# One list schedule for the whole kernel: order pinned on every engine, the halves of two chunks in turn, the positive part of the ELU on ScalarE

## The chip, the core and the metric

The kernel runs on one core of a Trainium2 chip. TensorE (PE in the profile) multiplies, VectorE (DVE), ScalarE (ACT) and GpSimd (POOL) work on tiles, and SyncE (SP) issues the DMAs. The metric is the device time of one execution in microseconds (us); the figure for a kernel is the median of its runs.

## The reference

Three stages follow one another, over 3072 tokens (4 sequences of 768) with 384 features (8 heads of 48):

```python
for t in range(S):                       # gated linear attention, per sequence and head
    state = alpha[t][:, None] * state + outer(k[t], v[t])
    y[t] = q[t] @ state
h = x @ w_in                             # 384 -> 2048
x2 = where(h > 0, h, exp(min(h, 0)) - 1) @ w_out
g = x2 @ w_gate; val = x2 @ w_val        # 384 -> 1536
out = (g * sigmoid(g) * val) @ w_out2
```

All of it is in single precision. The kernel reaches it with three passes per product (high by high, high by low, low by high) on operands that are split into a high and a low part.

## The kernel before, in words

The 768 steps are cut into 6 chunks of 128 steps. A chunk of all four sequences is a block of 512 tokens (TB), and one sequence's share of a chunk is a *unit* u = 0 to 23 (unit u belongs to chunk u // 4).

*Attention of a unit* (class `Attention`). `load` fetches one tile `in` of 1 MB with the decays F, K, Q and V; there are three such buffers, so unit u + 3 is fetched when unit u is done. `A` multiplies the decays up (a scan on DVE, four pieces), clamps them (`R`), and ACT takes the inverse by Ln and Exp. `N` and `M` scale K by a guarded inverse (the tile `N`) and Q by the decay; two of their products, K by `R` and Q by F, run on POOL (L214, L224), the others on DVE (L212, L222). `Dk` transposes K on PE (L235) and ACT keeps it as `KT`; `E` forms the scores on PE (L254) and DVE masks them into `A` (L261); `Gs` forms the new state on PE (L274, L278); `Hy` forms the outputs on PE (L299 from the state `sbd`, L304 and L308 from the scores), and ACT and DVE split them into the high and low part of `x` and of `x3`. After a chunk's fourth unit `gaps` fills the remaining rows of `x` from `x3` with six small DMAs.

*First layer* (`moe1`), for each chunk 16 steps f: nine products of 128x512 into `h` (`mm1`), the ELU on ACT and DVE (L361 to L367), whose result is split into the high and low part of `g`, and nine products into the three accumulators `acc` (`mm2`, two steps f later). *Second layer* (`moe2`), for each chunk 12 steps: 18 products into `gv`, the gate, and twelve products of 128x384 into `q`. All of these products are issued in `mm3` and so have line L117. Results of the first layer go through DRAM (`x2d`), and `load_split` brings them back.

*Weights* (class `Weight`) come in tiles of 768 KB of float64, 16 for the first layer and 18 for the second. A tile passes through one of two `raw` buffers: two conversions on ACT (L91, L93), two merges on DVE (L95, L98), and a split into high and low, one instruction on ACT (L105) and one on DVE (L106). One tile of the first layer is prepared at each step f of chunk 0, three before it.

*What sets the order.* The code emits the work in a fixed pattern: 30 products of zeros to begin with, the attention of chunk 0, then the first layer of chunk c with the attention of chunk c + 1 cut into 28 pieces and dealt out over its steps (`POPS`). From that the framework's scheduler (it simulates a timeline) makes each engine's order; it is free to move instructions of one engine past each other. Each engine then runs its list strictly in order.

Of the kernel before, what the change touches and what calls it, by code (L numbers as in the profile page):

```python
# [18 lines left out]
DM = H * D  # L19
# [13 lines left out]
AHEAD = 2  # L33
EARLY = 10
POPS = [3] * 9 + [1] + [0] * 6
PASSES = ((0, 0), (0, 1), (1, 0))


@with_exitstack
def kernel(  # L40
# [9 lines left out]
    nc = tc.nc  # L50

# [3 lines left out]
    def open_pools(es, weights):  # L55
        P.wp = es.enter_context(tc.tile_pool(name="wp", bufs=weights))
        P.xp = es.enter_context(tc.tile_pool(name="xp", bufs=2))
        P.ep = es.enter_context(tc.tile_pool(name="ep", bufs=2))
        P.gp = es.enter_context(tc.tile_pool(name="gp", bufs=3))
        P.rp = es.enter_context(tc.tile_pool(name="rp", bufs=AHEAD))  # L60
        P.op = es.enter_context(tc.tile_pool(name="op", bufs=2))

    dp = ctx.enter_context(tc.tile_pool(name="dp", bufs=1, space=bass.MemoryType.DRAM))
    x2d = [dp.tile([128, KD, TB], F32, name=f"x2d{c}") for c in range(NCH)]
# [10 lines left out]


    class Weight:


        def __init__(self, pool, tag, src):  # L80
            self.t = pool.tile([128, 2, WT], F32R, tag=tag, name="wt")
            self.raw = P.rp.tile([128, WT, 2], I32, tag="raw", name="raw")
            nc.sync.dma_start(
                out=self.raw.rearrange("p a t -> p (a t)"), in_=src.bitcast(I32))

        def value(self):
# [3 lines left out]
            lo, hi = self.raw[:, :, 0], self.raw[:, :, 1]  # L90
            nc.scalar.activation(  # L91
                out=hi.bitcast(F32), in_=hi.bitcast(F32), func=AF.Copy, scale=2.0 ** -112)
            nc.scalar.activation(  # L93
                out=lo, in_=lo.bitcast(U32), func=AF.Copy, scale=0.936 * 2.0 ** -29)
            nc.vector.scalar_tensor_tensor(  # L95
                out=lo, in0=hi, scalar=3, in1=lo,
                op0=ALU.logical_shift_left, op1=ALU.bitwise_or)
            nc.vector.scalar_tensor_tensor(  # L98
# [3 lines left out]
        def split(self):  # L102
            w = self.raw[:, :, 0].bitcast(F32)
            hi, lo = self.t[:, 0], self.t[:, 1]
            nc.scalar.activation(out=hi, in_=w, func=AF.Copy)  # L105
            nc.vector.tensor_tensor(out=lo, in0=w, in1=f32(hi), op=ALU.subtract)  # L106
            del self.raw
# [7 lines left out]
    def mm3(o, lhs, rhs, first, last):  # L115
        for i, (a, b) in enumerate(PASSES):
            nc.tensor.matmul(  # L117
                out=o, lhsT=lhs(a), rhs=rhs(b),
                start=first and i == 0, stop=last and i == 2,
            )  # L120


    class Attention:
        def __init__(self, es):
            self.cp = es.enter_context(tc.tile_pool(name="acp", bufs=1))
            self.p1 = es.enter_context(tc.tile_pool(name="ap1", bufs=1))
            self.p2 = es.enter_context(tc.tile_pool(name="ap2", bufs=2))
            self.p3 = es.enter_context(tc.tile_pool(name="ap3", bufs=3))
# [12 lines left out]
            self.turn = False  # L141

        def bank(self, u=NU):

            self.turn = not self.turn
            if u < B and not self.turn:
                return pacc.tile([128, 512], F32, tag="acc2", name="acc2")
            return self.ps.tile([128, 512], F32, tag="aps", name="aps")

        def pair(self, u):  # L150

            if u < B and u % 2 == 0:
# [21 lines left out]
        def warm(self, n):  # L174

            z = self.cp.tile([128, 128], BF16, name="wz")
            nc.vector.memset(z, 0.0)
            o = pacc.tile([128, 512], F32, tag="acc2", name="acc2")
            for _ in range(n):
                nc.tensor.matmul(  # L180
                    out=o, lhsT=z, rhs=z[:, None, :].to_broadcast([128, 4, 128]), start=True, stop=True)

        def load(self, u):
            t = self.p3.tile([128, 4, NP * C], F32, tag="in", name="in")
            for i, j in ((0, 1), (1, 4)) if u == 0 else ((0, 4),):
                nc.sync.dma_start(out=t[:, i:j], in_=qkva[u][:, i:j])
            f, k, q = (t[:, i].rearrange("p (a c) -> p a c", a=NP) for i in range(3))
            self.u[u] = dict(t=t, F=f, K=k, Q=q, v=t[:, 3].rearrange("p (h d) -> p h d", h=H))

        def A(self, u):  # L190

            d = self.u[u]
            for p in range(NP):
                f = d["F"][0:PR, p]
                nc.vector.tensor_tensor_scan(  # L195
                    out=f, data0=f, data1=self.zero[0:PR].to_broadcast([PR, C]),
                    initial=1.0, op0=ALU.mult, op1=ALU.add,
                )
            r = self.p1.tile([128, NP * C], F32, tag="R", name="R")[0:PR]
            nc.vector.tensor_scalar(  # L200
                out=r, in0=d["t"][0:PR, 0], scalar1=2.0 ** -60, scalar2=2.0 ** 60,
                op0=ALU.max, op1=ALU.min)
            nc.scalar.activation(out=r, in_=r, func=AF.Ln)
            nc.scalar.activation(out=r, in_=r, func=AF.Exp, scale=-1.0)  # L204
            d["R"] = r

        def N(self, u):

            d = self.u[u]
            t = self.p1.tile([128, NP * C], F32, tag="N", name="N")[0:PR]  # L210
            f, k = d["t"][0:PR, 0], d["t"][0:PR, 1]
            nc.vector.scalar_tensor_tensor(  # L212
                out=t, in0=f, scalar=0.0, in1=d["R"], op0=ALU.max, op1=ALU.mult)
# [514 lines left out]
```

## Time and profile before

| | us |
|---|---|
| median of 3 runs (1021.95 to 1024.06) | 1022.18 |
| the profiled execution | 1022.64 |
| its span, first to last instruction | 1020.9 |
| PE busy, of the span | 980.6 |
| DVE, ACT, POOL busy | 573.5, 462.7, 86.2 |

Line numbers are those of the code above. "busy" of PE is modelled and holds time in which products only wait in its pipeline, so a span at 100% need not be at full pace; the start of a group of nine products against the start of the next is the better measure. A row of the timeline gives start, duration, engine, line, operation, result and operands, and how many instructions it merges; in brackets is the idle time ahead and what ended it.

### The profile page before, as it was taken

Reading aid. Unit: us, or ns where it says so; the run is one execution under the profiler, and the core shown is the slowest. Engines: PE = TensorE matmul, PEld = TensorE weight load, DVE = VectorE, ACT = ScalarE, POOL = GpSimd, SP = SyncE. Lnnn points to the kernel's source line nnn. Section 1 sums busy time; section 2 is a strip of 40 time slices with the busy share of each in tenths; the row PEclk is TensorE's granted clock in tenths of the full one; section 3 lists DMA queues with packets and bytes.
Section 4 is the critical chain, followed back from the end, with each engine's and each line's share of the span. In section 5 each row is a group of like instructions: output and inputs, shape, how many; then the busy total and the mean of one; then the engine's idle time right before and its main releaser. Section 6 shows DMA issues by size and latency. Waiting matters only on the chain.

```text
span 1020.9 us, 13174 instructions
## 1 busy us (share of the span) xinstructions
PE 980.6 (96%) x5248; PEld 813.9 (80%) x5248; DVE 573.5 (56%) x951; ACT 462.7 (45%) x806; POOL 86.2 (8%) x59
## 2 busy tenths in 40 slices
PE   7589999999999999999998999999999999999997
PEld 4467778877787878888776888888888888888886
DVE  6899996656665665647888433433433433433332
ACT  5678786455555455637877321211311222212121
POOL 4223111120211121100000000000000000000000
PEclk8589999999999999999999999999999999999998
DMA  5544432222112212203533100100200100100001
GB/s 227 206 160 165 165 120 74 83 57 73 43 55 75 83 42 58 73 16 125 186 124 125 62 1 1 62 1 1 62 1 1 62 1 1 62 1 22 10 0 35
DMA packets 18934, 69.36 MB, mean 68 GB/s; under 512 B 2480, under 2 KB 5552, under 8 KB 15920
## 3 DMA queue, kind: packets, MB, share of 16 engines
q1 hardware_dynamic: 18864, 68.43, 19.9%
q8 instruction: 43, 0.70, 0.3%
q14 instruction: 27, 0.22, 0.1%
HBM read 56.62 MB, written 9.44 MB: 65 GB/s over the span
## 4 chain that ended last, share of the span: by engine, by line
PE 79%; DVE 8%; DMA 7%; ACT 3%; issue 2%; SPq 0%; POOL 0%; DVEq 0%
PE gv L117 29%; PE q L117 15%; PE acc L117 14%; PE h L117 14%; DMA raw<-w 4%; DMA in<-qkva 2%; PE ape L254 2%; DVE wt L106 2%; PE aps L299 2%; PE aps L308 1%; DVE raw L98 1%; DVE raw L95 1%; DVE in L195 1%; ACT raw L93 1%; ACT raw L91 1%
## 5 line engine op out<-in xcount | busy, mean ns | idle before, releaser
L117 PE MATMUL gv<-x,wt 128*128 128x512 f32 x1296 | 310.1, 393 | 2.3 <-DVE e L364 2.3
L117 PEld LDWEIGHTS gv<-x,wt 128*128 128x128 f32 x1296 | 243.3, 189 | 51.0 <-issue 2.7
L117 PE MATMUL acc<-g,wt 128*128 128x512 f32 x864 | 224.6, 398 | 4.3 <-DVE g L367 2.4
L117 PE MATMUL h<-x,wt 128*128 128x512 f32 x864 | 220.3, 398 | 8.4 <-DVE e L364 4.2
L117 PEld LDWEIGHTS h<-x,wt 128*128 128x128 f32 x864 | 161.3, 190 | 45.5 <-DVE e L364 6.6
L117 PEld LDWEIGHTS acc<-g,wt 128*128 128x128 f32 x864 | 158.7, 188 | 44.0 <-DVE g L367 4.4
L117 PE MATMUL q<-wt,u 128*128 128x384 f32 x864 | 163.0, 337 | 0.0
L117 PEld LDWEIGHTS q<-wt,u 128*128 128x128 f32 x864 | 153.6, 188 | 5.5
L414 DVE TENSOR_TENSOR s<-gv,s 128x512 f32<-128x512 f32 x72 | 49.8, 692 | 180.9 <-ACT s L413 180.8
L413 ACT ACTIVATE s<-gv 128x512 f32<-128x512 f32 x72 | 43.1, 598 | 185.3 <-PE gv L117 185.2
L416 ACT ACTIVATE u<-s 128x512 fp32r<-128x512 f32 x72 | 45.4, 631 | 130.4 <-DVE s L415 130.4
L366 ACT ACTIVATE g<-e 128x512 fp32r<-128x512 f32 x96 | 60.2, 629 | 65.6 <-DVE e L364 64.1
L361 ACT ACTIVATE e<-h 128x512 f32<-128x512 f32 x96 | 56.7, 590 | 58.7 <-PE h L117 57.8
L367 DVE TENSOR_TENSOR g<-e,g 128x512 fp32r<-128x512 f32 x96 | 67.8, 708 | 16.5 <-ACT g L366 15.0
L363 DVE TENSOR_SCALAR e<-e 128x512 f32<-128x512 f32 x96 | 42.6, 446 | 61.2 <-ACT e L362 61.0
L417 DVE TENSOR_TENSOR u<-s,u 128x512 fp32r<-128x512 f32 x72 | 49.8, 692 | 44.0 <-ACT u L416 44.0
L415 DVE TENSOR_TENSOR s<-gv,s 128x512 f32<-128x512 f32 x72 | 49.8, 691 | 43.0 <-PE gv L117 43.0
L364 DVE SCALAR_TENSOR_TENSOR e<-h,e 128x512 f32<-128x512 f32 x96 | 65.9, 687 | 2.1
L224 POOL TENSOR_TENSOR in<-in 112x512 f32<-112x512 f32 x24 | 40.6, 1691 | 300.2 <-DVE in L195 266.5
L362 ACT ACTIVATE e<-e 128x512 f32<-128x512 f32 x96 | 59.9, 628 | 1.8
L195 DVE TENSOR_TENSOR_SCAN in<-in,zero 112x128 f32<-112x128 f32 x96 | 34.5, 415 | 26.8 <-DMA in<-qkva 26.8
L214 POOL TENSOR_TENSOR in<-in,R 112x512 f32<-112x512 f32 x24 | 43.6, 1818 | 35.7 <-ACT R L204 35.6
(88 smaller groups left out, 776.0 us busy)
## 6 DMA issues: line engine op xcount, KB each, us to landing
raw<-w SPq DMA_DIRECT2D x34, 768.0 KB, 4.3
in<-qkva SPq DMA_DIRECT2D x23, 1024.0 KB, 5.0
x2d<-o SPq DMA_DIRECT2D x18, 256.0 KB, 2.0
x2r<-x2d SPq DMA_DIRECT2D x18, 256.0 KB, 2.9
out<-y SPq DMA_DIRECT2D x24, 192.0 KB, 2.0
x<-x SPq DMA_DIRECT2D x36, 64.0 KB, 4.5
in<-qkva SPq DMA_DIRECT2D x1, 768.0 KB, 5.1
in<-qkva SPq DMA_DIRECT2D x1, 256.0 KB, 3.7
```

Of the source, the lines that this page charges most:

```text
L117: nc.tensor.matmul(out=o, lhsT=lhs(a), rhs=rhs(b), start=first and i == 0, stop=last and i == 2,)
L195: nc.vector.tensor_tensor_scan(out=f, data0=f, data1=self.zero[0:PR].to_broadcast([PR, C]), initial=1.0, op0=ALU.mult, op1=ALU.add,)
L214: nc.gpsimd.tensor_tensor(out=k, in0=k, in1=d["R"], op=ALU.mult)
L361: nc.scalar.activation(out=e, in_=h, func=AF.Relu, scale=-1.0)
L362: nc.scalar.activation(out=e, in_=e, func=AF.Exp, scale=-1.0)
L364: nc.vector.scalar_tensor_tensor(out=e, in0=h, scalar=0.0, in1=e, op0=ALU.max, op1=ALU.add)
L366: nc.scalar.activation(out=g[:, 0], in_=e, func=AF.Copy)
L367: nc.vector.tensor_tensor(out=g[:, 1], in0=e, in1=f32(g[:, 0]), op=ALU.subtract)
L414: nc.vector.tensor_tensor(out=e, in0=ps[0], in1=e, op=ALU.mult)
L415: nc.vector.tensor_tensor(out=e, in0=ps[1], in1=e, op=ALU.mult)
L416: nc.scalar.activation(out=g[:, 0], in_=e, func=AF.Copy)
L417: nc.vector.tensor_tensor(out=g[:, 1], in0=e, in1=f32(g[:, 0]), op=ALU.subtract)
```

## The change

All work is listed first, as steps of a `Plan`, each with its engine, an estimated duration, the buffers that it reads and writes, and a mark `port` for those of DVE and POOL that are to exclude one another in the plan. `run` is a list scheduler: it takes the engine that can begin first, on it the ready step with the longest chain of work behind it (`tail`; attention's products on PE get 40 us on top, and are taken as ready 0.5 us late), and emits all steps in the order of their planned starts. `Pinned` makes each instruction of an engine depend on the one before it, so the framework's scheduler keeps that order.

Other parts: the first layer of chunks 0 and 1 is done in halves, in the order chunk 0 steps 0 to 7, chunk 1 steps 0 to 7, chunk 0 steps 8 to 15, chunk 1 steps 8 to 15; the sums of the first halves go to DRAM (`half`), come back (`part`), and are added on DVE. The list puts the attention of chunk 1 with the first of these segments, that of chunk 2 with the fourth. For units 0 to 3 the two products of POOL run on DVE. The mask of scores that lie in one tile is one instruction of 128x1024. In the ELU the positive part is a second Relu on ACT into a tile `r`, and DVE forms e - 1 + r in one instruction where it had two (the subtraction of 1, L363, is gone; L364 read `h` from PSUM, the new one reads two tiles in SBUF). The output buffers are three where they were two.

```diff
-POPS = [3] * 9 + [1] + [0] * 6
+HALF = NF1 // 2
+SEGMENTS = [(0, 0, HALF, 1), (1, 0, HALF, 0), (0, HALF, NF1, 0), (1, HALF, NF1, 2)]
+SEGMENTS += [(c, 0, NF1, (c + 1) % NCH) for c in range(2, NCH)]
+SOON, MARGIN = 40.0, 0.5
+RAWS, INS, OUTS, GS = 2, 3, 3, 3
...
+    def run(self):
...
+            t, eng, at = best
+            i = max((i for i in at if at[i] <= t), key=lambda i: (tail[i] + ops[i][5], -i))
+            ready[eng].remove(i)
+            start[i], free[eng] = t, t + ops[i][1]
+            if ops[i][4]:
+                port = free[eng]
...
+        for i in sorted(range(n), key=lambda i: (start[i], i)):
+            ops[i][2]()
...
+            ins = getattr(self.engine, name)(*a, **k)
+            if self.on:
+                if self.prev is not None:
+                    self.tc.add_manual_dep(
+                        ins.ins, self.prev, mybir.DependencyInfo(
+                            mybir.DependencyClass.NoSync, mybir.DependencyReason.DATA),
+                        reason="order of the plan")
+                self.prev = ins.ins.name
...
+        def helper(self, u):
+            return pool if u >= B else vec
+        def cost(self, u):
+            return ("POOL", 1.3) if u >= B else ("DVE", 0.62)
...
-            nc.vector.tensor_scalar(out=e, in0=e, scalar1=-1.0, scalar2=None, op0=ALU.add)
-            nc.vector.scalar_tensor_tensor(
-                out=e, in0=h, scalar=0.0, in1=e, op0=ALU.max, op1=ALU.add)
+            def pos():
+                d["r"] = P.ep.tile([128, TB], F32, tag="r", name="r", bufs=1)
+                act.activation(out=d["r"], in_=d["h"], func=AF.Relu)
+            def elu():
+                vec.scalar_tensor_tensor(
+                    out=d["e"], in0=d["e"], scalar=-1.0, in1=d["r"], op0=ALU.add, op1=ALU.add)
...
+            plan.add("PE", 2.05, product, r=[w1[f // G, 0].key, *xs], w=[hk, "chain"])
+            plan.add("ACT", 0.55, pos, r=[hk], w=["r"])
+            plan.add("DVE", 0.63, elu, r=["r"], w=[ek], port=True)
...
+    for c, f0, f1, n in SEGMENTS:
+        if n:
+            for u in range(B * n, B * n + B):
+                at.step(u)
...
+        for f in range(f0, f1):
+            if (f // G, 0) not in w1:
+                prep_w1(plan, f)
+                prep_w1(plan, f + 1)
+            mm1(f)
```

The order that results, at three places. In the changed kernel every instruction of the plan has line L123, that of the wrapper. A trailing "x4" is four instructions in one row.

First, DVE up to the last part of `x` that chunk 0's first product needs (the last row of each). Before:

```order
L261 TENSOR_TENSOR A_422<-ape_411,mask_119 128x512
L106 TENSOR_TENSOR wt_472<-raw_473,wt_472 128x768
L222 SCALAR_TENSOR_TENSOR in_320<-N_424,in_320 112x512
L319 TENSOR_TENSOR x3_123<-aps_372,x3_123 112x128
L320 TENSOR_TENSOR x_185<-aps_372,x_185 112x3x128
L95 SCALAR_TENSOR_TENSOR raw_503<-raw_503 128x768
L195 SCALAR_TENSOR_TENSOR in_385<-in_385,zero_120 112x128 x4
L98 SCALAR_TENSOR_TENSOR raw_503<-raw_503 128x768
L319 TENSOR_TENSOR x3_123<-acc2_441,x3_123 112x128
L320 TENSOR_TENSOR x_185<-acc2_441,x_185 112x3x128
```

and in the changed kernel:

```order
L123 SCALAR_TENSOR_TENSOR in_338<-in_338,zero_119 112x128 x4
L123 TENSOR_SCALAR R_397<-in_338 112x512
L123 TENSOR_TENSOR wt_376<-raw_178,wt_376 128x768
L123 TENSOR_TENSOR A_408<-ape_382,mask_118 128x1024
L123 TENSOR_TENSOR x3_122<-aps_366,x3_122 112x128
L123 TENSOR_TENSOR x_257<-aps_366,x_257 112x3x128
L123 SCALAR_TENSOR_TENSOR N_426<-in_338,R_397 112x512
L123 SCALAR_TENSOR_TENSOR in_391<-in_391,zero_119 112x128 x4
L123 TENSOR_TENSOR x3_122<-acc2_417,x3_122 112x128
L123 TENSOR_TENSOR x_257<-acc2_417,x_257 112x3x128
```

Up to that point stand 14 instructions on `raw` and `wt` before (five weight tiles begun), and 3 now (one tile, whose split is the row on `wt_376`); the eight products that POOL had for units 0 to 3 are among DVE's now.

Second, PE near the eighth step of chunk 0 (`x_185` and `x_257` are chunk 0's block, `x_569` chunk 1's; the name behind it is the weight tile). Before:

```order
L117 MATMUL h_1060<-x_185,wt_738 128x512 x9
L117 MATMUL acc0_479<-g_931,wt_683 128x512
L117 MATMUL acc1_480<-g_931,wt_683 128x512
L117 MATMUL acc2_481<-g_931,wt_683 128x512
L117 MATMUL acc0_479<-g_931,wt_683 128x512 x2
L117 MATMUL acc1_480<-g_931,wt_683 128x512 x2
L117 MATMUL acc2_481<-g_931,wt_683 128x512 x2
L117 MATMUL h_1103<-x_185,wt_875 128x512 x9
L254 MATMUL ape_1322<-in_762 128x128
L117 MATMUL acc0_479<-g_994,wt_808 128x512
```

and in the changed kernel:

```order
L123 MATMUL h_947<-x_257,wt_823 128x512 x9
L123 MATMUL acc0_607<-g_923,wt_859 128x512 x3
L123 MATMUL acc1_608<-g_923,wt_859 128x512 x3
L123 MATMUL acc2_609<-g_923,wt_859 128x512 x3
L123 MATMUL h_985<-x_569,wt_376 128x512 x9
L123 MATMUL acc0_607<-g_964,wt_982 128x512 x3
L123 MATMUL acc1_608<-g_964,wt_982 128x512 x3
L123 MATMUL acc2_609<-g_964,wt_982 128x512 x3
```

After eight steps chunk 0 needs a new weight tile before (`wt_875`); now chunk 1 begins there with the first tile (`wt_376`), which has been ready since the start. Its own second half needs the next tiles sixteen groups of products later.

Third, the scores of a unit on PE (a result `ape`). Before, those of unit 7 stand in three pieces among products:

```order
L254 MATMUL ape_1322<-in_762 128x128
L117 MATMUL acc0_479<-g_994,wt_808 128x512
L117 MATMUL acc1_480<-g_994,wt_808 128x512
L117 MATMUL acc2_481<-g_994,wt_808 128x512
L254 MATMUL ape_1322<-in_762 128x128
L235 MATMUL aps_904<-ident_118,in_595 128x112 x4
L117 MATMUL acc0_479<-g_994,wt_808 128x512 x2
L117 MATMUL acc1_480<-g_994,wt_808 128x512 x2
L117 MATMUL acc2_481<-g_994,wt_808 128x512 x2
L254 MATMUL ape_1322<-in_762 128x128 x6
```

and in the changed kernel:

```order
L123 MATMUL acc0_607<-g_750,wt_693 128x512 x3
L123 MATMUL acc1_608<-g_750,wt_693 128x512 x3
L123 MATMUL acc2_609<-g_750,wt_693 128x512 x3
L123 MATMUL h_809<-x_257,wt_657 128x512 x9
L123 MATMUL aps_826<-ident_117,in_567 128x112 x4
L123 MATMUL ape_834<-in_567 128x128 x8
L123 MATMUL aps_849<-in_567,KT_843 64x48
```

They are one piece now, beside the transposition of the same unit. From the first product of the first layer on, attention stands in 78 pieces between products before, and in 53 now.

## Rows read from the trace of the kernel before

**Rows 1.** Windows by stage: length; busy PE, PEld, DVE, ACT, POOL; clock; DMA.

```profile
0.00:56.10 56.10, 34.37 (x255) 23.94 (x255) 45.27 (x83) 34.99 (x61) 19.45 (x22) 0.67 0.55 201
56.10:157.10 101.00, 97.52 (x582) 76.67 (x583) 94.16 (x154) 80.07 (x139) 20.62 (x11) 0.96 0.45 152
157.10:243.20 86.10, 86.10 (x521) 68.83 (x520) 54.68 (x105) 47.43 (x92) 15.37 (x8) 1.00 0.21 67
...
415.60:496.50 80.90, 78.53 (x417) 62.81 (x416) 51.30 (x86) 48.04 (x79) 2.98 (x2) 1.00 0.24 79
496.50:565.10 68.60, 63.31 (x262) 49.02 (x261) 55.47 (x81) 54.29 (x82) 0.00 (x0) 0.98 0.40 138
565.10:1013.50 448.40, 448.39 (x2161) 394.63 (x2159) 164.38 (x243) 103.16 (x173) 0.00 (x0) 1.00 0.06 20
1013.50:1020.90 7.40, 0.00 (x0) 0.00 (x0) 0.69 (x2) 0.37 (x1) 0.00 (x0) 0.65 0.33 115
```

**Rows 2.** Timeline of PE: the first product, one after a stall, two undisturbed.

```profile
56.09 2.90 PE L117 MATMUL h<-x,wt 128*128 128x512 f32 x6 [3.93 <-DMA x<-x]
...
79.78 3.64 PE L117 MATMUL h<-x,wt 128*128 128x512 f32 x9 [1.57 <-DVE e L364]
...
474.75 2.20 PE L117 MATMUL h<-x,wt 128*128 128x512 f32 x9
476.79 2.20 PE L117 MATMUL acc<-g,wt 128*128 128x512 f32 x9
```

**Rows 3.** Window of DVE alone, first scan to chunk 0's last part of x.

```profile
4.60:53.20 48.60, 42.23 (x73) 0.65 0.56 211
```

**Rows 4.** Timeline of DVE, an undisturbed stretch of chunk 0's attention.

```profile
41.77 0.94 DVE L106 TENSOR_TENSOR wt<-raw,wt 128x768 fp32r<-128x768 f32 x1
42.64 0.94 DVE L98 SCALAR_TENSOR_TENSOR raw<-raw 128x768 int32<-128x768 int32 x1
43.51 0.67 DVE L212 SCALAR_TENSOR_TENSOR N<-in,R 112x512 f32<-112x512 f32 x1
44.11 1.27 DVE L261 TENSOR_TENSOR A<-ape,mask 128x512 int32<-128x512 int32 x2
45.31 0.94 DVE L106 TENSOR_TENSOR wt<-raw,wt 128x768 fp32r<-128x768 f32 x1
```

**Rows 5.** Timeline of DVE beside work of POOL.

```profile
11.78 1.52 DVE L200 TENSOR_SCALAR R<-in 112x512 f32<-112x512 f32 x1
...
203.16 0.66 DVE L364 SCALAR_TENSOR_TENSOR e<-h,e 128x512 f32<-128x512 f32 x1
...
255.62 1.76 DVE L212 SCALAR_TENSOR_TENSOR N<-in,R 112x512 f32<-112x512 f32 x1
```

**Rows 6.** Timeline of POOL at the same three places.

```profile
11.76 1.26 POOL L224 TENSOR_TENSOR in<-in 112x512 f32<-112x512 f32 x1 [2.09 <-DVE in L195]
...
203.47 1.29 POOL L224 TENSOR_TENSOR in<-in 112x512 f32<-112x512 f32 x1 [14.21 <-DVE in L195]
...
255.54 1.29 POOL L214 TENSOR_TENSOR in<-in,R 112x512 f32<-112x512 f32 x1 [1.06 <-ACT R L204]
```

**Rows 7.** Timeline of PE, scores in a piece of two and in one piece.

```profile
264.21 0.49 PE L254 MATMUL ape<-in 48*128 48x128 f32 x2
264.62 2.34 PE L117 MATMUL acc<-g,wt 128*128 128x512 f32 x9
...
273.43 1.16 PE L254 MATMUL ape<-in 48*128 48x128 f32 x16
274.52 0.50 PE L117 MATMUL acc<-g,wt 128*128 128x512 f32 x1
```

**Rows 8.** The page's costliest groups: count, busy, mean ns, idle before.

```profile
L361 ACT ACTIVATE e<-h 128x512 f32<-128x512 f32 x96 | 56.7, 590 | 58.7 <-PE h L117 57.8
L214 POOL TENSOR_TENSOR in<-in,R 112x512 f32<-112x512 f32 x24 | 43.6, 1818 | 35.7 <-ACT R L204 35.6
```

**Rows 9.** Waits: engine and line, what for; us in total, times, longest.

```profile
DVE in L195 <- DMA in<-qkva: 26.8, 17, 3.6
```

More of the change, by code (lines that the diff above doesn't have):

```diff
@@ L50 @@
     nc = tc.nc
+    vec, act, pool, ten, syn = engines = [
+        Pinned(tc, e) for e in (nc.vector, nc.scalar, nc.gpsimd, nc.tensor, nc.sync)]
     class P:
@@ new lines, in split_lo @@
+        def split_lo():
+            vec.tensor_tensor(
+                out=w.t[:, 1], in0=w.raw[:, :, 0].bitcast(F32), in1=f32(w.t[:, 0]),
+                op=ALU.subtract)
+        plan.add("SP", 0.5, load, w=[hk, lk], kb=768)
+        plan.add("ACT", 0.82, high, w=[hk])
+        plan.add("ACT", 0.82, low, w=[lk])
+        plan.add("DVE", 0.88, merge, r=[hk], w=[lk], port=True)
+        plan.add("DVE", 0.88, sign, r=[hk], w=[lk], port=True)
+        plan.add("ACT", 0.82, split_hi, r=[lk], w=[w.key])
@@ L109, in as_cols @@
+        plan.add("DVE", 0.88, split_lo, r=[lk], w=[w.key], port=True)
+        return w
     def as_cols(w):
@@ new lines, in E, with scores @@
+                plan.add("ACT", 0.65, state, r=[("sc", b)], w=[("sbd", u % 2)])
+            keys, pair = self.pair(u)
+            def scores():
+                d["s"] = o = pair()
+                for p in range(NP):
+                    for j in range(2):
+                        r = slice(64 * j, 64 * j + D)
+                        ten.matmul(
+                            out=(o[j] if len(keys) > 1 else o[:, j])[:, p * C:(p + 1) * C],
+                            lhsT=d["K"][r, p], rhs=d["Q"][r, p], start=True, stop=True,
+                        )
@@ L267, in Gs @@
+            plan.add("PE", 1.25, scores, r=[K, Q], w=keys, soon=SOON, lag=MARGIN)
+            plan.add("DVE", 1.24 if len(keys) > 1 else 1.1, causal, r=keys, w=["A"])
         def Gs(self, u):
@@ L401, in mm_gv, with low, moe2 @@
+            def low(m=m, o=o):
+                vec.tensor_tensor(
+                    out=b.t[:, 1, m], in0=o.t, in1=f32(b.t[:, 0, m]), op=ALU.subtract)
+            plan.add("SP", 0.5, load, r=[(after, m)], w=[o.key])
+            xk = ("x", c % 2, m)
+            plan.add("ACT", 0.55, high, r=[o.key], w=[xk])
+            plan.add("DVE", 0.63, low, r=[o.key], w=[xk], port=True)
+        return b
+    def moe2(plan, x, xs, w2, pools, yp, put):
+        accs, us = {}, {}
         def mm_gv(f):
-            fs = slice((f % G) * 128, (f % G) * 128 + 128)
@@ new lines, in low @@
+            def low():
+                vec.tensor_tensor(
+                    out=d["g"][:, 1], in0=d["e"], in1=f32(d["g"][:, 0]), op=ALU.subtract)
+            plan.add("ACT", 0.55, sigmoid, r=[gks[0]], w=[ek])
+            plan.add("DVE", 0.63, lambda: times(0), r=[gks[0]], w=[ek])
+            plan.add("DVE", 0.63, lambda: times(1), r=[gks[1]], w=[ek])
+            plan.add("ACT", 0.57, high, r=[ek], w=[uk])
+            plan.add("DVE", 0.63, low, r=[ek], w=[uk], port=True)
+            us[f] = d, uk
```

794 lines of the change are left out of this document (468 added, 326 removed).

## The prediction, as it was made

> **What bounds the kernel now.** I read the busy shares by stage first, then PE's timeline where a stage begins, then DVE's timeline in the stage that looked worst. The stages [rows 1] are, with their lengths: the attention of chunk 0 ahead of any product of the first layer, 56.1 us; chunk 0's first layer with the attention of chunk 1, 101.0; chunks 1, 2 and 3, of which one row stands and which take 86.1, 86.2 and 86.2; chunk 4, 80.9; chunk 5, 68.6; the second layer, 448.4; and 7.4 behind it for the last output. They add up to the span of 1020.9; the execution has 1.7 us around it (1022.6), and the median of the runs is 0.5 below the profiled one.
>
> A group of nine products takes 2.04 us when nothing disturbs it (from 474.75 to 476.79) [rows 2]. The second layer takes 448.4 us with PE never free, and its order is the same in the change (18 products of `gv`, twelve of `q`): nothing is to be had there. Chunks 1 to 3 are PE's too: 32 groups make 65.3 us, the attention of four units the other 20.9, 5.2 a unit. Chunk 0 does the same work on PE in 101.0 us, 14.9 more; there DVE is busy for 94.2 of the 101.0, and in chunk 1 for 54.7 of 86.1. In the first 56.1 us PE has only attention and the clock is 0.67 of full speed in the mean, and DVE again has little left: it is busy for 42.2 of the 48.6 us [rows 3] between its first scan and the last part of `x`, at 53.2; the first product starts 2.9 us after that [rows 2]. In chunks 4 and 5 PE is free for 2.4 and 5.3 us [rows 1], because ACT and DVE prepare the second layer's weights there. So the kernel is DVE's for 157 us and PE's for nearly all of the rest.
>
> **The start.** What DVE does up to the last part of `x` changes like this (counts from the two orders, durations as steps from start to start in an undisturbed stretch [rows 4]):
> - Eleven weight instructions go behind it (14 become 3): 11 x 0.87 = 9.6 us less.
> - Eight products of POOL come to DVE. The trace does not show them there; the nearest row is the `N` of L212, also two tiles of 112x512 in SBUF, 0.60. That adds 4.8. From both sides: by the weights' 0.87 it would be 7.0, by half of the two mask instructions' 1.20, 0.60 again.
> - One product of the next unit goes behind: 0.6 less.
> - Collisions with POOL go. The clamp of 11.78 took 1.52 us and ended 0.28 us after the POOL instruction that had begun at 11.76 and took 1.26 [rows 5, 6]; it is the first of six instructions of DVE that are stretched so in this part, by 0.7 to 1.1 us, 5.6 together.
>
> 42.2 - 9.6 + 4.8 - 0.6 - 5.6 = 31.2 us of work. DVE's waits in the stretch, 48.6 - 42.2 = 6.4 us, are for ACT, PE and loads; I leave them as they are, since the chain of a unit through ACT and a PE at low clock stays and fewer fillers stand between. Then `x` is ready at 4.6 + 31.2 + 6.4 = 42.2 and the first product starts at 45.1 instead of 56.1: **-11.0 us**. Without any wait it would be 38.7 (-17.4); if the waits grow by what the work shrinks, nothing is won. POOL's idleness costs nothing there.
>
> **Chunk 0.** DVE now has, from 42.2 up to the fifth pair of `e` and `g` (from where on a step needs only that pair and a few weights), 20 weight instructions (17.4), ten of the ELU (6.0, priced as L212) and 18.7 of attention, priced alike: 42.1 us, ending at 84.3. PE's own work up to the same place is 11 groups, 22.5, and nearly four units, about 19: from 45.1 to 86.6. Without disturbance PE just sets the end. DVE has disturbances: of the 101.0 us before, 6.8 were idle and collisions of that kind with POOL's 11 products [rows 1], ten of 0.2 to 1.1 us, cost 7.6, together 14%; at that rate 42.1 becomes 49.0, the fifth pair is ready at 91.2, and PE waits for 5. Afterwards chunk 1's first half needs no new weight, and the eight tiles for the second halves spread over 66 us of products. So of the 14.9 us about 5 stay: **-9.9 us**, between -14.9 and 0.
>
> The ELU itself loses one DVE instruction (L363) and has one more on ACT, 0.59 us [rows 8]; 96 of them are 57 us on an engine that is busy for 80.1 of 101.0 us in chunk 0 and for 47.4 of 86.1 in chunk 1 [rows 1]. There it is hidden by PE. In chunk 0 the eight steps of the first segment bring ACT 4.7 us while it loses weights of the later tiles, so I count it as nothing; without cover it is 0.1 us a step, the difference of 0.59 and the subtraction that it replaces, at most 5 us on 48 steps. The twelve DMAs and six additions of the halves (one addition like a `g`, about 0.7 us) lie beside PE and a DMA share of 0.21 [rows 1]: nothing, at most 4 us if PE waited for all six additions.
>
> The new instruction reads two tiles in SBUF where L364 read `h` in PSUM. The trace shows what that exposes it to: L364 took 0.66 us beside a POOL instruction, L212, with two SBUF operands, 1.76 beside another, against 0.67 alone [rows 4 to 6]. The Trainium skill says the same (GPSIMD Engine Reference, § 8 Key points): POOL shares its SBUF interfaces with VectorE and contends with instructions that read two SBUF inputs or run in a two-port mode. By that rule each of the 40 POOL products left could hold one ELU for 1.1 us, 44 us of DVE in all. I do not add them to the sum, as the subtraction that goes was open to the same; they enter the slow rival.
>
> **Pieces.** Products of the first layer are now in whole groups. Scores in a piece of two records took 0.41 us from their start to the next group's, 16 in one piece 1.09 [rows 7]: by its share a piece of two would take 0.14, so cutting off a piece costs some 0.27. From chunk 1 on there are 41 pieces instead of 59: 18 x 0.27 = **-4.9 us**; 0 if the cost belonged to the scores alone, -7 at the whole 0.41.
>
> **Chunks 4 and 5.** PE's free 7.7 us. Before, all 18 tiles of the second layer stand ahead of its first gate on DVE; now ten do, and the rest lies among the gates, where DVE is busy for 164 of 448 us. I give back **-5**, between -7.7 and +4 (a gate queued on DVE behind a late weight; a step of 6.2 us holds about 3 us of DVE work).
>
> Sum: -11.0 - 9.9 - 4.9 - 5 = -30.8; span 990.1, execution 991.8, and 0.5 less for the median: 991.4, so **991 us**.
>
> **Rivals.**
> - *DVE never sets the end* (0.20). No collisions from POOL at the start, and the list puts urgent work first, so the 5 us of chunk 0 and the 6.4 us of waits go too: 980 us. Against it: DVE strictly keeps its list, so each late operand holds everything behind it.
> - *The start does not move* (0.21). The chain of a unit (scan, ACT, product, PE, mask, PE) or the loads, for which scans waited 17 times and 3.6 us at worst [rows 9], set chunk 0's attention, and the eight products that come to DVE lie in that chain. Then the first term is gone: 1002; with chunk 0 no better either, 1012.
> - *The plan's margins are too small* (0.08), the slow side. Attention's products on PE are put 0.5 us behind the planned end of their inputs and ahead of everything else. The plan has 1.3 us for a POOL product that took 1.82 in the mean [rows 8]; two of them and a collision of 1.1 [rows 5] make a unit 2.1 us late, 1.6 after the margin, and PE, whose list is now fixed, waits. For 20 units that is 32 us. After a stall PE came back at a lower clock: 3.64 us for nine products after 1.57 us idle [rows 2], 1.6 more; for one unit in four, 8 us. In all 1031. It decides from 1.6 us a unit on. Against it: POOL's products of a unit have a whole unit's time, some 13 us, in advance, and two thirds of DVE are free from chunk 1 on.
> - That the order is not what it says is excluded, since the built program shows it.
>
> **How the numbers follow.** The forecast has 0.51. My range for it alone is 984 to 998; with the rivals 978 to 1012, which leaves out the slow one and the ends of the fast one. Within 0.2% (about what can be told from no change here, 2 us) lies only what is between the slow rival and the partial ones: 0.03. Faster 0.90, slower 0.07.
>
> **What will show it.** First product at 43 to 48 us, and the last part of `x` on DVE 3 us ahead of it; chunk 0's first segment with PE waiting for `e` or `g` or a weight for about 5 us; chunk 2 on at 84 to 86 us a chunk; chunk 5 near 65; second layer 448. I am wrong if PE idles before the scores or `Gs` in every unit, if the first product still starts after 52, or if the gates of the second layer's first chunk wait for weights.

## The result, and the profile after

The changed kernel takes 991.94 us (median of 4 runs, 987.93 to 993.67), the kernel before 1022.34 (4 runs): a ratio of 0.9694, 95% interval 0.9659 to 0.9729. The profiled execution of after took 990.41, its span 988.6; that of before 1022.64 and 1020.9. One run of one later kernel, the old ELU with the load behind, took 1012.51 at a granted clock of 0.936 and is left out of its median.

The windows by stage of the kernel after answer to [rows 1]; the columns are the same. The first ends at chunk 0's first product, the fourth begins at the first product that chunk 2 adds to `acc`, the sixth at that of chunk 5; the seventh is the second layer.

```profile
0.00:43.00 43.00, 28.43 (x258) 19.93 (x259) 36.20 (x79) 27.60 (x53) 7.21 (x15) 0.81 0.60 210
43.00:96.50 53.50, 47.43 (x346) 37.65 (x346) 49.19 (x80) 45.77 (x82) 11.75 (x7) 0.96 0.60 196
96.50:235.20 138.70, 138.56 (x873) 112.68 (x873) 107.76 (x166) 110.71 (x207) 23.56 (x14) 1.00 0.40 134
235.20:400.40 165.20, 164.50 (x998) 133.66 (x996) 95.77 (x155) 106.18 (x205) 22.87 (x15) 1.00 0.19 60
400.40:471.20 70.80, 70.80 (x356) 58.68 (x353) 27.68 (x44) 40.47 (x75) 2.41 (x1) 1.00 0.05 10
471.20:531.70 60.50, 59.93 (x264) 48.89 (x263) 40.83 (x56) 52.49 (x84) 0.00 (x0) 1.00 0.38 127
531.70:981.20 449.50, 448.45 (x2159) 394.25 (x2159) 188.02 (x271) 124.55 (x199) 0.00 (x0) 1.00 0.10 34
981.20:988.60 7.40, 0.51 (x3) 0.19 (x2) 0.62 (x2) 0.49 (x1) 0.00 (x0) 0.80 0.34 117
```

Stretches of the two kernels can't be set against each other as they stand, because the list brings attention forward. The groups of PE's scores, after from 43.0 to 235.2, and before over its stretch to nearly the same place (56.1 to 243.2: the same 288 products of `acc`, two of `h` fewer), show it: 160 products, ten units, against 128, eight.

```profile
L123 PE MATMUL ape<-in 48*128 48x128 f32 x160 | 11.6, 285 | 0.0
```

```profile
L254 PE MATMUL ape<-in 48*128 48x128 f32 x128 | 12.6, 294 | 0.0
```

A unit costs PE 4.5 us in the changed kernel (in chunk 2 of its timeline a group of `h` starts at 290.38, the one behind a whole unit at 301.04; three groups of 2.04 lie between), so two units are 9.1 us. With that moved back, the 32.3 us of span are as follows (the forecast's pieces are shared out by units, its 5 us for chunks 4 and 5 by their idle time of 2.4 and 5.3):

| stretch | before | after, same work | difference | forecast |
|---|---|---|---|---|
| to the first product | 56.1 | 43.0 | -13.1 | -11.0 |
| to chunk 2's first `acc` | 187.1 | 192.2 - 9.1 | -4.0 | -9.9 and -1.2 of the pieces |
| to chunk 5's first `acc` | 253.3 | 236.0 + 9.1 | -8.2 | -3.7 of the pieces, -1.6 of chunk 4 |
| to the second layer | 68.6 | 60.5 | -8.1 | -3.4 of chunk 5 |
| second layer and tail | 455.8 | 456.9 | +1.1 | 0 |

At the start, DVE alone over the stretch that answers to [rows 3], and rows of its timeline (the second unit's clamp, the last part of `x`, an `N` of the first segment) with POOL's at the `N`:

```profile
4.50:38.50 34.00, 31.61 (x67) 0.82 0.63 235
```

```profile
11.40 0.43 DVE L123 TENSOR_SCALAR R<-in 112x512 f32<-112x512 f32 x1
...
37.74 0.72 DVE L123 TENSOR_TENSOR x<-acc,x 112x128 fp32r<-112x128 f32 x2
...
58.46 1.79 DVE L123 SCALAR_TENSOR_TENSOR N<-in,R 112x512 f32<-112x512 f32 x1
```

```profile
57.77 1.93 POOL L123 TENSOR_TENSOR in<-in,R 112x512 f32<-112x512 f32 x1 [3.57 <-ACT R L123]
```

DVE has 31.6 us of work up to the last part of `x` (42.2 before) and 2.4 of waits (6.4 before). The clamp that took 1.52 beside POOL [rows 5] takes 0.43; where POOL works again, an `N` is still held, and ends 0.55 us behind it.

PE's timeline: the first product, the first of chunk 1, and the second layer's first `q`; and SP's issues around the gaps of chunks 0 and 1.

```profile
43.03 4.13 PE L123 MATMUL h<-x,wt 128*128 128x512 f32 x9 [0.17 <-ACT R L123]
...
96.56 2.30 PE L123 MATMUL h<-x,wt 128*128 128x512 f32 x9 [3.43 <-DMA x<-x]
...
540.67 0.62 PE L123 MATMUL q<-wt,u 128*128 128x384 f32 x2 [0.59 <-ACT u L123]
541.75 2.01 PE L123 MATMUL q<-wt,u 128*128 128x384 f32 x10 [0.46 <-DVE u L123]
```

```profile
38.54 3.94 SPq L123 DMA_DIRECT2D x<-x  x6
42.59 0.52 SPq L123 DMA_DIRECT2D in<-qkva  x1
...
86.85 0.33 SPq L123 DMA_DIRECT2D in<-qkva  x1
89.52 3.82 SPq L123 DMA_DIRECT2D x<-x  x6
```

The second layer's 1.1 us more are the two waits of its first `q`. The first segment's only long wait is for the six small DMAs that fill chunk 1's gaps; a 1 MB load went out ahead of them, which it did not at chunk 0.

### The profile page after: what moved, and what is told of

Same layout as the page of the kernel before. It is cut to its first block, busy times and chain, and to the rows that moved or that the text cites. A ratio compares the mean times of both kernels' runs of the same rounds, so it can differ in the third digit from the quotient of the medians.

```text
span 988.6 us, 13147 instructions
## 1 busy us (share of the span) xinstructions
PE 958.6 (97%) x5248; PEld 805.9 (82%) x5248; DVE 546.1 (55%) x847; ACT 508.3 (51%) x902; POOL 67.8 (7%) x51
## 4 chain that ended last, share of the span: by engine, by line
PE 86%; DVE 6%; DMA 3%; ACT 3%; issue 1%; SPq 0%; DVEq 0%; ACTq 0%
PE gv L123 29%; PE h L123 18%; PE acc L123 18%; PE q L123 15%; PE aps L123 4%; DMA in<-qkva 2%; PE ape L123 2%; DVE in L123 2%; DVE raw L123 1%; DMA raw<-w 1%; ACT raw L123 1%; DVE wt L123 1%; DVE N L123 1%; DVE A L123 1%; DMA x<-x 1%
## 5 line engine op out<-in xcount | busy, mean ns | idle before, releaser
L123 PE MATMUL gv<-x,wt 128*128 128x512 f32 x1296 | 308.1, 391 | 0.0
L123 PEld LDWEIGHTS gv<-x,wt 128*128 128x128 f32 x1296 | 242.2, 188 | 48.0
L123 PE MATMUL h<-x,wt 128*128 128x512 f32 x864 | 216.8, 395 | 3.6 <-DMA x<-x 3.4
L123 PE MATMUL acc<-g,wt 128*128 128x512 f32 x864 | 216.3, 394 | 1.3 <-DVE g L123 1.3
L123 DVE TENSOR_TENSOR s<-gv,s 128x512 f32<-128x512 f32 x144 | 99.5, 691 | 212.7 <-ACT s L123 170.5
L123 PEld LDWEIGHTS h<-x,wt 128*128 128x128 f32 x864 | 161.3, 189 | 39.1 <-ACT wt L123 3.8
L123 PEld LDWEIGHTS acc<-g,wt 128*128 128x128 f32 x864 | 159.7, 188 | 38.3 <-DVE g L123 2.4
L123 PE MATMUL q<-wt,u 128*128 128x384 f32 x864 | 163.4, 337 | 1.1 <-ACT u L123 0.6
L123 PEld LDWEIGHTS q<-wt,u 128*128 128x128 f32 x864 | 153.4, 188 | 7.3 <-ACT u L123 1.0
L123 ACT ACTIVATE s<-gv 128x512 f32<-128x512 f32 x72 | 42.9, 596 | 175.2 <-PE gv L123 175.1
L123 DVE SCALAR_TENSOR_TENSOR e<-e,r 128x512 f32<-128x512 f32 x96 | 67.5, 703 | 96.1 <-ACT r L123 95.8
L123 ACT ACTIVATE u<-s 128x512 fp32r<-128x512 f32 x72 | 45.4, 631 | 111.9 <-DVE s L123 111.5
L123 ACT ACTIVATE e<-h 128x512 f32<-128x512 f32 x96 | 56.9, 593 | 64.6 <-PE h L123 64.0
L123 DVE TENSOR_TENSOR g<-e,g 128x512 fp32r<-128x512 f32 x96 | 68.6, 714 | 27.4 <-ACT g L123 27.2
L123 ACT ACTIVATE g<-e 128x512 fp32r<-128x512 f32 x96 | 60.5, 630 | 39.4 <-DVE e L123 39.3
L123 DVE SCALAR_TENSOR_TENSOR raw<-raw 128x768 int32<-128x768 int32 x68 | 66.1, 976 | 13.6 <-ACT raw L123 13.0
L123 DVE TENSOR_TENSOR u<-s,u 128x512 fp32r<-128x512 f32 x72 | 49.8, 692 | 36.1 <-ACT u L123 35.6
L123 ACT ACTIVATE raw<-raw 128x768 f32<-128x768 f32 (+1 forms) x68 | 59.3, 906 | 8.1 <-DMA raw<-w 7.9
L123 ACT ACTIVATE e<-e 128x512 f32<-128x512 f32 x96 | 60.6, 632 | 2.9
L123 ACT ACTIVATE r<-h 128x512 f32<-128x512 f32 x96 | 55.8, 581 | 0.0
L123 POOL TENSOR_TENSOR in<-in 112x512 f32<-112x512 f32 x20 | 32.1, 1603 | 227.0 <-DVE in L123 206.0
L123 DVE TENSOR_TENSOR_SCAN in<-in,zero 112x128 f32<-112x128 f32 x96 | 33.9, 415 | 14.6 <-DMA in<-qkva 14.5
```

Of the source, the lines that this page charges most:

```text
L123: ins = getattr(self.engine, name)(*a, **k)
```

## The experiments

Twelve kernels, the median of 5 or 6 runs each; "the list" is the order that the plan makes. Differences are against after (991.94) unless another kernel is named.

**No halves.**

```diff
-SEGMENTS = [(0, 0, HALF, 1), (1, 0, HALF, 0), (0, HALF, NF1, 0), (1, HALF, NF1, 2)]
-SEGMENTS += [(c, 0, NF1, (c + 1) % NCH) for c in range(2, NCH)]
+SEGMENTS = [(c, 0, NF1, (c + 1) % NCH) for c in range(NCH)]
```

> The changed kernel without halves: chunk 0 does its 16 steps in one stretch, as every chunk does; list, pinning and all else stay. Forecast's theory (the halves spare DVE the later weight tiles while the attention of chunk 1 runs): DVE then has 45 weight instructions (39 us) instead of 20 (17 us) to do beside PE's first 18 groups or so, so PE waits 5 to 9 us more in chunk 0: 996 to 1000 us. Rival (the list's order alone removes chunk 0's excess, the halves only add six additions and twelve DMAs): 988 to 993.

1001.41 (999.82 to 1003.94; ratio to before 0.9789, 0.9771 to 0.9807): 9.5 slower, the theory's direction and a little over its range. From its first product to the second layer's it took 497.4 us (44.44 to 541.88) against 488.7. All the rest of the change together is worth 21 us of the gain, the halves 9.5.

The theory's reason is not what the trace shows: PE waits for weights for 1.5 us in chunk 0, not for 5 to 9. It waits for attention and, at chunk 1's first product, for the gaps as after does, and behind both waits its clock is at the lower level, 1.2 GHz (0.50 from 107 to 110 and from 138 to 142):

```profile
105.31 0.67 PE L122 MATMUL aps<-in,KT 128*64 128x48 f32 x16 [1.48 <-ACT KT L122]
106.65 3.60 PE L122 MATMUL acc<-g,wt 128*128 128x512 f32 x8 [0.24 <-DVE g L122]
138.29 4.18 PE L122 MATMUL h<-x,wt 128*128 128x512 f32 x9 [4.29 <-DMA x<-x]
```

Eight products take 3.40 us to the next group where 1.81 is the pace, and the group, the transposition and the scores from 138.29 on take 6.55 (to 144.84) where 3.61 is: 4.5 of the 9.5. Another 1.4 is the later first product, and some 1.6 are unit 4's transposition and scores, which stand behind that product here and ahead of it in after. No run has whole chunks with the load of the next experiments out of the way.

**POOL at the start.**

```diff
-            return pool if u >= B else vec
+            return pool
-            return ("POOL", 1.3) if u >= B else ("DVE", 0.62)
+            return ("POOL", 1.3)
```

> The changed kernel with the two products of units 0 to 3 on POOL again. Forecast's theory (4.8 us of work that came to DVE against 5.6 us of collisions that went; the weights moved behind are the bulk of the gain): first product at 42 to 46 us, total 990 to 994. Rival A (collisions at the start are the main loss of before): first product at 48 or later, 996 or more. Rival B (the eight products are a pure load on DVE): first product at 38 to 40, 985 to 988.

999.50 (0.9774, 0.9760 to 0.9788), first product at 50.79: the forecast's theory falls, and the numbers are rival A's. DVE alone up to its last part of `x`, and one of eight instructions that POOL stretches there, by 6.6 us together, with POOL's beside it:

```profile
4.50:44.30 39.80, 35.93 (x63) 0.70 0.55 207
```

```profile
23.52 1.76 DVE L123 SCALAR_TENSOR_TENSOR N<-in,R 112x512 f32<-112x512 f32 x1
```

```profile
22.99 1.74 POOL L123 TENSOR_TENSOR in<-in,R 112x512 f32<-112x512 f32 x1 [4.80 <-ACT R L123]
```

The work is 4.3 us more than in after: 4.8 less for the products, 6.6 for the collisions, 2.6 for three weight instructions that the list fits in here. Waits are 1.5 more, and the first product comes another 2.0 later. So the forecast priced a collision rightly (5.6 us for six), and as an exchange against eight products on DVE that is 1.8; the other 6 of the 7.8 us are what the list and the waits made of it (the six small DMAs land in 4.3 us in the median here, in 2.4 in after). So that collisions are the main loss, rival A's reason, is not shown.

**The old ELU, and a load out of the way.** The first kernel has the ELU of before (first diff), the second a load behind the small DMAs (second diff), the third has both.

```diff
-            plan.add("ACT", 0.55, pos, r=[hk], w=["r"])
-            plan.add("DVE", 0.63, elu, r=["r"], w=[ek], port=True)
+            plan.add("DVE", 0.35, less, w=[ek], port=True)
+            plan.add("DVE", 0.63, elu, r=[hk], w=[ek])
```

```diff
-                plan.add("SP", 0.5, lambda: alloc(0, 4), w=[F, K, Q, V], kb=1024)
+                plan.add("SP", 0.5, lambda: alloc(0, 4), r=behind, w=[F, K, Q, V], kb=1024)
-                self.load(u + INS)
+                self.load(u + INS, [("x", c % 2, B)] if b == B - 1 else [])
```

> The changed kernel with the ELU of before (a subtraction of 1 and one instruction that reads h from PSUM on DVE, no second Relu on ACT). Forecast (the ELU's edit is worth nothing): 990 to 993. Rival A (DVE sets the end in the first segment, each of its eight steps gets 0.35 us longer there): first segment 3 us longer, 993 to 996. Rival B (the new instruction's two tiles in SBUF collide with POOL): 986 to 989.

997.71 (0.9762, 0.9743 to 0.9782), over both rivals, and not for the reason of either: the first product was late, before any ELU had run. SP's and PE's timelines:

```profile
37.55 0.33 SPq L123 DMA_DIRECT2D in<-qkva  x1
39.48 4.30 SPq L123 DMA_DIRECT2D x<-x  x6
```

```profile
48.45 4.18 PE L123 MATMUL h<-x,wt 128*128 128x512 f32 x9 [4.65 <-DMA x<-x]
```

> The changed kernel, where the list puts the load of a unit that becomes free with a chunk's last unit behind the six small DMAs that fill the gaps of x. In the changed kernel that load of 1 MB goes out 2.7 us ahead of chunk 1's six, whose median landing is then 4.7 to 5.1 us against 2.4 us at chunk 0, and PE waits 3.43 us for them. Theory (the load delays the small ones): that wait falls to 0.5 to 1.5 us, total 988 to 990. Rival (the last unit's work on DVE sets when they go out): the wait stays over 2.5 us, 991 to 993.

990.20 (989.21 to 991.00; 0.9676, 0.9659 to 0.9693). The wait fell as the theory said, and the median landing of chunk 1's six DMAs from 5.1 to 2.5 us; the total cannot be told from after's.

PE's first product of chunk 1, and the six DMAs there (each KB, median us to landing):

```profile
95.48 2.51 PE L123 MATMUL h<-x,wt 128*128 128x512 f32 x9 [1.07 <-DMA x<-x]
```

```profile
x<-x SPq DMA_DIRECT2D x6, 64.0 KB, 2.5
```

> The ELU of before as in the run with the ELU alone, and the load behind the small DMAs. There the first product came at 48.45 us instead of 43.03, with the same work on DVE and a 1 MB load 1.9 us ahead of the six small DMAs, which took 7.0 us instead of 2.4. Theory (that load, not the ELU, cost those 5.4 us): first product at 43 to 44, total 990 to 994. Rival (the ELU costs by itself): first product still after 47, or total 996 and more.

994.16 (five runs; 0.9721, 0.9702 to 0.9740), first product at 44.16 against 44.08 in the kernel with the load behind: the load had cost the start, as the theory said. What is left, 4.0 us against that kernel, is the ELU's: the subtraction takes DVE 0.44 us a step (its group is below), and by chunk 1's first product (97.81 against 95.48) the old one is 2.3 us late.

```profile
L123 DVE TENSOR_SCALAR e<-e 128x512 f32<-128x512 f32 x96 | 42.6, 443 | 85.7 <-ACT e L123 85.4
```

**Scores in pieces.**

```diff
-            plan.add("PE", 1.25, scores, r=[K, Q], w=keys, soon=SOON, lag=MARGIN)
+                for p in range(NP):
+                    plan.add("PE", 0.31, lambda p=p: scores(p, p + 1), r=[K, Q], w=keys, soon=SOON,
+                             lag=1.0 if p else MARGIN)
```

> The changed kernel with the scores of units 8 to 23 listed as four pieces of four products, each at least 1 us behind the one before, so that products of the first layer stand between: 84 pieces of attention from the first product on instead of 53. Forecast's theory (cutting off a piece costs 0.27 us): 31 x 0.27 = 8.4 us, 1000. Rival A (the records of scores, not the cuts, cost that): 991 to 993. Rival B (the mask, and with it the outputs, come late and PE waits): over 1004, with idle time of PE ahead of the outputs.

1004.79 (0.9823, 0.9802 to 0.9843), 12.9 more, over the theory's 8.4. The waits did not grow, so rival B is out. There are 48 more pieces of scores (three more for each of 16 units; 17 of them beside other attention, which the expectation had not counted): 0.27 each by the medians, and 0.34 by the profiled executions, where the first layer took 504.9 us instead of 488.7. PE's timeline shows both sides of the price: a piece of four takes 0.42, where a quarter of 1.09 is 0.27, and the group behind it 2.17, not 2.04.

```profile
323.67 0.49 PE L123 MATMUL ape<-in 48*128 48x128 f32 x4
324.09 2.34 PE L123 MATMUL h<-x,wt 128*128 128x512 f32 x9
326.26 2.20 PE L123 MATMUL acc<-g,wt 128*128 128x512 f32 x9
```

**All of the second layer's tiles first** (18 instead of 10 ahead of the first gate).

```diff
+                every = [w.key for w in w2.values()] if f == 0 else []
-                plan.add("PE", 2.05, product, r=[w2[f // G, s].key, *xs], w=[gks[s], "chain"])
+                plan.add("PE", 2.05, product, r=[w2[f // G, s].key, *xs, *every], w=[gks[s], "chain"])
```

> The changed kernel with all 18 tiles of the second layer prepared ahead of its first gate, as before the change (in the changed kernel 10). Forecast's theory (that is why PE was free for 7.7 us in chunks 4 and 5): PE waits 5 to 10 us more in chunk 5 or ahead of the first gate, 997 to 1002. Rival (the order on ACT and DVE, not the count, made it free): 991 to 994.

992.61 (989.07 to 996.57; 0.9711, 0.9688 to 0.9733): the rival. PE waits 2.8 us in chunk 5 instead of 0.6, but the second layer starts at 531.80 against 531.76.

**Weights ahead of the first product** (with the load behind, against 990.20).

```diff
+            every = [w.key for w in w1.values()] if f == f0 == 0 else []
-            plan.add("PE", 2.05, product, r=[w1[f // G, 0].key, *xs], w=[hk, "chain"])
+            plan.add("PE", 2.05, product, r=[w1[f // G, 0].key, *xs, *every], w=[hk, "chain"])
```

> The kernel of the run with the load behind, where chunk 0's first product also reads the first four weight tiles, so that all four are ready ahead of it (in the changed kernel one is, and half of the others' work done). Forecast's theory of the start (weight instructions ahead of the first product are paid at 0.87 us each): six more of them, first product at 48 to 50. What that makes of the whole: as DVE is busy for 49 of 53 us in the first segment, work moved ahead is work saved there, 990 to 993. Rival (the first segment has room and the start counts in full): 995 to 997.

994.43 (0.9719, 0.9695 to 0.9743), 4.2 more, between the two ranges. The first product came 13.0 us later, for the list then put attention of unit 4 ahead of it as well; chunk 1's first is 6.4 later, the end 4.2. Most of the late start, with the work that was moved ahead of it, is given back, but not all. PE's timeline at both products:

```profile
57.11 7.21 PE L123 MATMUL h<-x,wt 128*128 128x512 f32 x27
...
101.92 2.37 PE L123 MATMUL h<-x,wt 128*128 128x512 f32 x9 [0.61 <-DMA x<-x]
```

**Who is bound to the list.** Three kernels with the same list, emitted in the same order; only the engines whose instructions each depend on the one before differ.

```diff
-        self.tc, self.engine, self.prev, self.on = tc, engine, None, True
+        self.tc, self.engine, self.prev, self.on = tc, engine, None, False
```

(`engine is not tc.nc.tensor` in place of `False` in the second, `engine is tc.nc.tensor` in the third.)

> The changed kernel with the same list, emitted in the same order, but no instruction bound to the one before it: the framework's scheduler orders each engine. On PE 121 runs of the first layer's products are then no whole groups, against 17, and five weight instructions stand ahead of the last part of x instead of one. Theory (whole groups are worth time): the 104 extra cuts at 0.05 to 0.1 us and 3.5 us at the start make 996 to 1004. Rival (what counts is what the list emits first; order within an engine is noise): 988 to 993.

1049.57 (1.0250, 1.0226 to 1.0274): 57.6 slower than after, and slower than before; the theory had the direction and a fifth of the size. In the trace DVE has 15 weight instructions ahead of the last part of `x`, against 3, and the first product starts at 62.96.

> The changed kernel where all engines but PE are bound to the list; PE's order is the framework's, 74 runs of the first layer's products in it are no whole groups, against 17 (121 in the run with all engines free, which was 58 us slower). Theory A (on PE the cuts are what costs, 0.1 to 0.4 us each): 57 more are 6 to 23 us, 998 to 1014, first product still at 43 to 45. Theory B (the order on DVE and ACT, which brings weights ahead of attention at the start, is what cost 58 us): 990 to 995.

1013.44 (0.9909, 0.9884 to 0.9934), 21.5 slower, first product at 43.91: theory A's numbers. But cuts are only part of it: from 40 to 560 us PE idles 18.7, in after 8.7. The waits are for steps that the list had timed, as this of PE (in total, times, longest), which after does not have:

```profile
PE h L123 <- ACT r L123: 6.9, 6, 2.2
```

> The complement of the run with PE's order free: only PE is bound to the list, DVE, ACT, POOL and SP have the framework's order; PE's 17 cuts are those of the changed kernel. All free cost 57.6 us, PE alone free 21.5. Theory A (the two add up: DVE's and ACT's order, with weights ahead of attention at the start, is the larger part): first product at 58 to 63, total 1020 to 1030. Theory B (the order on the other engines hurts only together with PE's): total under 1005, first product under 50.

1031.54 (1.0085, 1.0065 to 1.0106), 39.6 slower, first product at 59.29: theory A, a little over its range; 21.5 + 39.6 is 61.1, near the 57.6. The six small DMAs land in 5.5 us (median) here, in 2.4 in after. DVE, with no collision to speak of but 14 weight instructions ahead of the last part of `x`, needs the same time for it as before the change [rows 3]:

```profile
4.50:53.10 48.60, 42.54 (x80) 0.66 0.54 198
```

**Fillers** (with the load behind, against 990.20): 40 small products of zeros at the lowest priority (the list counts 0.27 us for each; eight in a row took 1.90).

```diff
+                for _ in range(n):
+                    plan.add("PE", 0.27, self.filler, r=[key], w=[self.wk], soon=-1e6)
```

> The kernel of the run with the load behind, with 40 small products of zeros (0.27 us each at full clock) listed on PE behind the state and output products of units 0 to 3 at the lowest priority, so that PE does not sit idle for 2 to 4 us there. In the changed kernel the pieces after such idle time ran at half clock (scores 2.08 us instead of 1.16, first group of the first layer 4.13 instead of 2.20 or so). Theory (that clock is on the path): first group at 42 to 43.5 with 2.0 to 2.2 us to the next, total 986 to 989. Rival (DVE sets the end of the first segment, PE's pace in it does not): 989 to 991.

989.27 (986.67 to 993.12; 0.9681, 0.9653 to 0.9708): inconclusive. The clock (the third column from the right in PE's windows) was at its upper level, 2.4 GHz, up to 43 us, where after has the lower one from 36 to 47; but PE then waited 2.2 us for the gaps and its first group ran at the lower level all the same.

```profile
40.00:43.00 3.00, 0.79 (x15) 1.00 0.62 101
43.00:44.00 1.00, 0.97 (x3) 0.61 1.24 178
44.00:45.00 1.00, 1.00 (x4) 0.50 0.40 131
```

PE's first group, and SP's six DMAs that it waited for:

```profile
43.03 3.88 PE L123 MATMUL h<-x,wt 128*128 128x512 f32 x9 [2.24 <-DMA x<-x]
```

```profile
38.48 3.96 SPq L123 DMA_DIRECT2D x<-x  x6
```

This and the kernel with the load behind have the lowest medians, but neither can be told from the changed kernel.

## Why the prediction was right, and where it was not

The total came out at the forecast, 991.9 for 991, and each term had the right sign. Two of the four had the wrong size, and they made up for one another: chunk 0 gave 6 us less, chunks 4 and 5 some 5 more. That the total was met so closely is luck in that part.

*The start* (-11.0; -13.1). The sum of DVE's work holds to 0.4 us: 31.2 forecast, 31.6 measured. That the waits would stay at 6.4 was wrong; they fell to 2.4. The gap between the last part of `x` and the first product went from 2.9 to 4.6. PE's list has unit 4's transposition and scores there, from 39.87 to 42.86, but they do not set it: with the fillers PE was idle for 2.2 us at that place, waiting for the six small DMAs, and the product started at the same 43.03. From the first of the six to the product it is 4.5 us in both, and 3.3 before (this row of SP, product at 56.09); why it grew, no run takes apart.

```profile
52.78 4.00 SPq L337 DMA_DIRECT2D x<-x  x6
```

Both causes are shown by runs: with the order of all engines but PE free, 14 weight instructions stand ahead and the 48.6 us of before are back; with POOL at the start 5.8 of them are. The rule weighed in the forecast (the Trainium skill, GPSIMD Engine Reference, § 8 Key points) holds: with POOL back at the start the collisions are back. The row that the forecast took for an operand in PSUM, `L364` at 203.16, began 0.31 us ahead of POOL's and could show nothing; this one of the kernel before can, where the `N` right behind it is held and it is not:

```profile
421.55 0.68 DVE L364 SCALAR_TENSOR_TENSOR e<-h,e 128x512 f32<-128x512 f32 x1
422.14 1.25 DVE L212 SCALAR_TENSOR_TENSOR N<-in,R 112x512 f32<-112x512 f32 x1
```

```profile
421.54 1.30 POOL L214 TENSOR_TENSOR in<-in,R 112x512 f32<-112x512 f32 x1
```

The rule's far side, 1.1 us for each of 40 ELUs, did not come, by the page's groups for the ELU and for `N`:

```profile
L123 DVE SCALAR_TENSOR_TENSOR e<-e,r 128x512 f32<-128x512 f32 x96 | 67.5, 703 | 96.1 <-ACT r L123 95.8
L123 DVE SCALAR_TENSOR_TENSOR N<-in,R 112x512 f32<-112x512 f32 x24 | 27.0, 1124 | 5.4 <-ACT R L123 5.4
```

The ELU's mean is 703 ns, `N`'s 1124 against 0.67 us alone. An ELU is exposed too (one at 67.70 took 1.05 us), but few meet a product of POOL; `N` waits for the same step of ACT as the product of L214 [rows 4, 5, 8] and meets it half the time.

*Chunk 0* (-9.9; -4.0). The step that failed is "chunk 0 does the same work on PE in 101.0 us, 14.9 more". It does more. The groups of before in chunk 0's and in chunk 1's stretch:

```profile
L117 PE MATMUL h<-x,wt 128*128 128x512 f32 x162 | 43.8, 417 | 6.7 <-DMA x<-x 3.9 <-DVE e L364 2.6
L254 PE MATMUL ape<-in 48*128 48x128 f32 x80 | 7.6, 293 | 0.0
```

```profile
L117 PE MATMUL h<-x,wt 128*128 128x512 f32 x151 | 38.6, 395 | 0.0
L254 PE MATMUL ape<-in 48*128 48x128 f32 x48 | 5.0, 295 | 0.0
```

Eleven products of `h` more (2.5 us) and the scores of two units (2.2) are work that stays: at least 4.7 of the 14.9 were never to be had. Nor was the rest DVE's alone: PE was idle for 3.5 of the 101.0 us [rows 1]. Of what is left PE still idles 6.1 in the first segment, as much as the 5 forecast, but not for `e`, `g` or a weight: 3.4 for chunk 1's gaps, 2.7 for attention. The first group at the lower clock is 2 us more. The halves are worth 9.5 by the run without them, but not by the forecast's way: its waits for weights are 1.5. The ELU's edit, priced as nothing in its own paragraph and counted with `L363` gone in this one, is worth 4.0.

*Pieces* (-4.9). The price holds: 0.27 us by the medians, 0.34 by the profiled executions, which for 18 pieces is 4.9 to 6.1.

*Chunks 4 and 5* (-5; about -10: 8.1 in chunk 5, and chunk 4's 2.4 of idle time, of which none is left). The term took the idle time alone and named the count of tiles ahead of the first gate. The run with all 18 ahead shows that the count costs 2 us of idle time and no total that can be told. Chunk 5's 29 groups take 59.2 us; before had 9.4 over that, of which idle time was 5.3, and after has 1.3. The other 4 lie at the same waits: PE has no other work there that cuts the products, and away from the waits the groups keep 2.04. The last wait shows part of it in the timeline of before:

```profile
555.44 3.69 PE L117 MATMUL acc<-g,wt 128*128 128x512 f32 x15 [0.30 <-DVE g L367]
561.42 6.62 PE L117 MATMUL gv<-x,wt 128*128 128x512 f32 x21 [2.28 <-DVE e L364]
```

The 21 products behind it take 6.45 us to the next row where 4.76 is the pace, the first of them at the lower clock (0.50 from 563.0 to 565.1). With DVE and ACT free but PE bound, PE idled 3.2 us in chunk 5, so part of the 5.3 may be their order; this was not taken apart further.

*The rivals.* That DVE never sets the end (980) is out: the ELU's 4.0 us show it. That the start does not move (1002, 1012) is out with the first product at 43.0. The slow one (margins too small) did not come: behind the first segment PE waits for nothing of attention.

## What to carry to other kernels

An order is worth what binds it: the same list, left to a scheduler that may reorder, was slower than the kernel it replaced, through cuts and waits on PE and through unurgent work ahead of urgent work on in-order engines, which added up. Before an excess over "the same work" is booked as a gain, count the instructions in both stretches; and price a stretch by its whole excess, not by its idle time alone, since what followed some of the waits was slow too. When one edit shifts the start of everything, look first at what else the list moved: here a load in front of six small DMAs looked like the price of an ELU.

## What the runs showed of the hardware

- Six DMAs of 64 KB landed in 2.4 to 2.5 us (median) with nothing ahead of them, and in 5.1 and 7.0 with a 1 MB load issued 2.7 and 1.9 us before.
- Cutting scores out of a stream of products costs 0.27 to 0.34 us a piece on PE with no idle time shown: the piece takes 0.42 where its share is 0.27, and the groups beside it 2.17 to 2.27 instead of 2.04.
- A DVE instruction on tiles in SBUF that met one of POOL ended 0.3 to 0.6 us behind it: `N` at 25.28, POOL at 24.73 (the two rows with POOL at the start); the first clamp there at 13.82, POOL at 13.54. An `N` that began 0.04 us ahead of POOL's product (152.97 in after) took 0.69, and the product 2.41 instead of 1.29.
- Behind waits of 1.48 and 4.29 us (the run without halves) and 2.28 (chunk 5 of before) PE ran at the lower clock; after the 4.29 a group of nine took 3.97 us to the next row instead of 2.04. Behind the wait of 3.43 us at 96.56 in after the clock stayed at 1.00, and the group took 2.14.
